# New slots for weight loads, weight splits and attention read-backs in a fused attention and feed-forward kernel

## The chip, the core and the metric

The kernel runs on one core of one Trainium2 chip. The core has a matrix engine (TensorE, PE in the profile, whose weight loads are a row of their own, PEld), a vector engine (DVE), an activation engine (ACT), a general engine (POOL) and an engine that issues most transfers (SP); 16 DMA engines move the data. The metric is the device time of the whole program in microseconds. All engines run their own instruction lists in order and wait for each other by semaphores, so the order of the instructions on each engine is part of the kernel.

## The reference

For 2048 tokens of width 576 the output is `x` plus an attention part plus a feed-forward part, both from the same normalised `x`:

```
xn = layernorm(x)
q, k, v = split(xn @ wqkv)                  # 32 heads of 18
# each token looks at 8 tokens: itself and those 2, 4, ... 14 before it
o = softmax(q . k_window * 18**-0.5) . v_window
out = x + o @ wo + relu(xn @ w1) @ w2       # w1: 576 x 4608, w2: 4608 x 576
```

Everything is float32. Since a token sees only tokens of its own parity, the even and the odd tokens are two independent problems up to the weights.

## The kernel before

**Tiling.** The program makes two phases, `ph` 0 and 1, one for each parity of 1024 tokens. In a phase the normalised tokens stand transposed in four tiles `XT` of 256 tokens (`xt_in` reads such a tile for phase 1, three transfers by `words_in`, L395 and L397; `xt_parts` splits it, L422 to L428). Each float32 operand is cut into a high and a low part, and a product is made of three: `two` writes the high part on ACT (L172) and the low part on DVE (L176) or, with `pooled`, on POOL (L174).

**Feed-forward.** The 4608 hidden columns are 36 blocks of 128. The first six come in two chunks `c` of three (`w1_load`, L188 and L193, brings one block `f` of a chunk with one transfer for 512 of the 576 rows and two for the last 64; `w1_split` cuts it). They are multiplied slot by slot: `h_two` makes the hidden values of one slot, `o_two` multiplies them with `w2`. The other 30 blocks are taken in 15 pairs by a Strassen scheme: a pair is two groups `g` of the 30 (`a` and `a + 1`), and each group has eight steps (`group`, `step`), in which TensorE alternates between hidden values (L163, `ph` and `pm`) and the product with `w2` (L163 or L142, `po`). A finished output piece is copied out of PSUM by ACT (L709, `ev`) and added to the output in DRAM by an accumulating transfer that POOL issues (L715, for rows of `wo` L718). `w2_load` (L207) brings a block of `w2` into one of two stage buffers `st2`, and `w2_split` cuts it in two halves; a load waits until the block two before it has been cut.

**Attention.** The heads go in four units of eight. Their products stand at groups 5, 11 and 17 (unit 0 in the slots before), the scores and sums run on DVE in the background (`bg`, `run_bg`). At the end of a unit DVE transposes the result (`o_turn`, L611 and L614) and SP writes it to DRAM (`o_out`, L619, four transfers). After the fourth unit the whole row block is read back as operands for `wo`: `ot_in` (L661, L663; three transfers for each of four row blocks `r0` to `r3`), `ot_split` (L670 on ACT, L671 and L672 on DVE; two halves for each block), and `wo_block` multiplies one block with `wo`. The rest of `wo` itself comes by `wo_rest` (L257, L260).

**What sets the order.** One Python pass writes all instructions. `on(ph, g, i, z, f)` hangs a call on step `i` of group `g`, "T" right behind the step's first matmuls, "O" behind its second ones; `at`, `first` and `late` do the same for slots. `run_bg` takes background work as far as a clock that the program itself keeps (`t["pe"]`, `t["dve"]`) leaves room. `ot_plan` makes a list of the read-back's calls, each with a condition and a distance in that clock to an earlier call, and `ot_go` takes the first that is allowed. Between the phases stands `seam()`: the last group of phase 0 (`tail_end`, `last_group`), the first slots of phase 1, and the multiplications with `wo`. After phase 1 `epilogue()` does the same without a successor. Nothing is reordered later; SP in particular issues transfers strictly in this order, and it waits with an issue when its buffer is not free or its data not there.

The calls around the change, in `plan_strassen` and `attention`:

```
on(ph, a - 1, 5, "O", w2_load, ph, f)
on(ph, a - 1, 6, "O", w2_load, ph, f + 1)
on(ph, a, 2, "O", w2_split, ph, f, (0,), True)
on(ph, a, 5, "T", w2_split, ph, f, (1,), True)
bg.append((NI * 160 + 150, o_turn, ()))
bg.append((0, o_out, ()))
```

Of the kernel before, what the change touches and what calls it, by code (L numbers as in the profile page):

```python
# [19 lines left out]
P = 128  # L20
# [50 lines left out]
def tile_body(ctx: ExitStack, tc: tile.TileContext, x, wqkv, wo, w1, w2, out):  # L71
# [112 lines left out]

    def w1_load(ph, c, f):
        st = ST[:, 640 * f : 640 * (f + 1)]
        cs = slice((c * C + f) * P, (c * C + f + 1) * P)
        nc.sync.dma_start(  # L188
            st[:, 0:512].rearrange("p (k c) -> p k c", k=KT),
            w1[0 : KT * P, cs].rearrange("(k p) c -> p k c", p=P),  # L190
        )
        for part in LOW, UPP:
            nc.sync.dma_start(st[part, 512:640], w1[KT * P : D, cs])  # L193

    def w1_split(ph, c, f, pooled=False):
        w = W1[ph, c, f] = w1_at(ph, c, f)
        two(w[:, 0, :], w[:, 1, :], ST[:, 640 * f : 640 * (f + 1)], 640, pooled)

# [336 lines left out]

    bg = deque()
    ready = {}

# [4 lines left out]
    def attention(ph, u):  # L543
# [498 lines left out]
    def plan_strassen(ph):  # L1042
        for p in range(NP):
            a = 2 * p
            f = NC0 * C + 2 * p
            if p:
# [32 lines left out]
        if ph == 0:  # L1079
            for i in range(2):  # L1080
                on(ph, NG - 1, 4 + i, "O", xt_in, 1, i)
            for i in range(2):
                on(ph, NG - 1, 8, "O" if i else "T", xt_parts, 1, i, 0)
                on(ph, NG - 1, 8, "O", xt_parts, 1, i, 1)
            on(ph, NG - 2, 6, "O", w1_load, 1, 0, 0)
            on(ph, NG - 2, 8, "O", w1_load, 1, 0, 1)
            on(ph, NG - 1, 2, "O", w1_load, 1, 0, 2)
            on(ph, NG - 2, 7, "O", w2_load, 1, 0)
            on(ph, NG - 1, 4, "O", w2_load, 1, 1)
            on(ph, NG - 1, 3, "O", w2_split, 1, 0, (0, 1), True)  # L1090
            on(ph, NG - 1, 6, "O", w1_split, 1, 0, 0, True)
            on(ph, NG - 1, 7, "O", w1_split, 1, 0, 1)

    OTQ, OTT = {}, {}

    def ot_plan(ph):
        z = OTQ[ph] = []
        done = lambda: ph in ready and t["pe"] > ready[ph] + 4.5
        free = lambda: done() and ("xs", ph) in hold
        z.append(("wl", wo_rest, (ph,), lambda: ph in ready, ()))  # L1100
# [77 lines left out]
    def group(ph, g):  # L1178
# [13 lines left out]
        def step(i, lower, upper, after, early=()):  # L1192
# [19 lines left out]
            fire(ph, g, i, "O")  # L1212
            ot_go(ph)
            for f, a in ins.pop((ph, g, i), ()):
# [58 lines left out]
    def seam():  # L1273
        ph, g, b = 0, NG - 1, BASE[1]

        def more(k):
            ot_go(0)
            if k == 2:
                for i in range(2, NTB):
                    xt_in(1, i)  # L1280
            elif k == 3:
                w2_load(1, 2)

        tail_end(0, more)
# [13 lines left out]
        w1_split(1, 0, 2, True)  # L1298
        w2_split(1, 2, pooled=True)
        wo_block(0, 0)  # L1300
# [14 lines left out]
    def epilogue():  # L1315
        ph = 1

        def more(k):
            ot_go(1)

# [48 lines left out]
    for ph in range(NPH):  # L1369
        b = BASE[ph]  # L1370
        for k in range(2 * NTB):
# [3 lines left out]
            qkv_slots.add(n)  # L1375
        for n, f in ((4, 0), (5, 1), (7, 2)):
            at(b + n, w1_load, ph, 1, f)
        for n, f in ((6, 0), (8, 1), (10, 2)):
# [26 lines left out]
        else:  # L1405
            for k in range(4):
                late(b + (0, 1, 3, 4)[k], xt_parts, 1, 4 + k, 0)
                late(b + (0, 1, 3, 4)[k], xt_parts, 1, 4 + k, 1)
            first(b + 3, wo_block, 0, 1)
# [31 lines left out]
    nc.scalar.activation(spare, mhalf, AF.Exp)  # L1441
    w1_load(0, 0, 0)
    load_x(2)
    w1_load(0, 0, 1)
    w1_load(0, 0, 2)
    w2_load(0, 0)
# [90 lines left out]
    for ph in range(NPH):  # L1537
        b = BASE[ph]
        for n in range(b + (FIRST if ph == 0 else 0), b + NOLD - 2):
# [5 lines left out]
            else:  # L1545
                h_two(g, n % 2 == 1)
            for f, a in todo.pop(n, []):
                f(*a)
# [11 lines left out]
        epilogue() if ph else seam()  # L1560
    assert not todo and not todo_late and not bg and not evs and not ins and not OTQ[0] and not OTQ[1]

# [25 lines left out]
```

## Time and profile before

| | |
|---|---|
| runs | 1141.21, 1142.63, 1145.81 us; median 1142.63 us |
| profiled execution | 1141.19 us, its span 1139.4 us, mean granted clock 0.993 |
| TensorE busy | 1112.4 us, 98% of the span |
| weight loads | 1097.7 us, 96% |
| VectorE, ACT, POOL | 75%, 50%, 34% |
| all DMA traffic | 177.27 MB, mean 156 GB/s |

A page of the profile is read from the span down: an engine that is busy 98% of the time bounds the kernel, and only its idle time and its slow clock can be won without taking work away. Times in the rows are microseconds from the span's start. In the rows of a timeline the last bracket says how long an engine stood idle ahead of the instruction and what ended the wait. "PEclk" is the clock that TensorE was granted, as a share of the full one. Phase 0 fills about the first half of the span; its last group begins near 514, and the last group of phase 1 near 1078.

### The profile page before, as it was taken

What the parts mean: (1) busy time and instruction counts of PE and PEld (TensorE: products, weight loads), DVE (VectorE), ACT (ScalarE), POOL (GpSimd) and SP (SyncE); (2) the same over time, 40 slices, a digit from 0 to 9 for tenths busy, and PEclk for the clock granted to TensorE, in tenths of its full rate; (3) what the DMA queues carried; (4) which work ended last, traced back from release to release, by engine and by line L of the source; (5) the groups of instructions that cost most, each with busy time, mean ns of one, the idle gap of its engine ahead of it and who ended that gap; (6) DMA issues with size and microseconds to landing.
All of it is one profiled execution on the core that took longest, in us unless ns stands there. A gap on an engine that the chain in (4) does not pass through costs nothing.

```text
span 1139.4 us, 37981 instructions
## 1 busy us (share of the span) xinstructions
PE 1112.4 (98%) x16410; PEld 1097.7 (96%) x16410; DVE 850.2 (75%) x1249; ACT 569.2 (50%) x1348; POOL 385.8 (34%) x382
## 2 busy tenths in 40 slices
PE   8999999999999999999999999999999999999988
PEld 8999999999999999998899999999999999999888
DVE  7676888898897898964316339987899989989441
ACT  4444564564464456656435245535645644655550
POOL 2313441343343344432212215333413423445221
PEclk9999999999999999999999999999999999999999
DMA  7469985794696498899857257759848947888885
GB/s 221 146 156 227 189 172 96 159 205 86 141 214 120 104 197 147 155 197 271 172 83 168 32 125 169 138 84 216 171 80 171 203 90 159 163 152 152 195 161 136
DMA packets 140727, 177.27 MB, mean 156 GB/s; under 512 B 28160, under 2 KB 88064, under 8 KB 140528
## 3 DMA queue, kind: packets, MB, share of 16 engines
q0 software_dynamic: 37632, 81.40, 45.6%
q1 hardware_dynamic: 102208, 92.55, 28.0%
q8 instruction: 129, 2.11, 0.7%
q10 hardware_dynamic: 720, 0.89, 0.2%
q14 instruction: 38, 0.31, 0.1%
HBM read 74.07 MB, written 96.22 MB: 149 GB/s over the span
## 4 chain that ended last, share of the span: by engine, by line
PE 85%; DVE 5%; DMA 4%; ACT 3%; issue 2%; SPq 1%; DVEq 0%; ACTq 0%; POOL 0%
PE po L163 28%; PE po L142 21%; PE ph L163 14%; PE pm L163 11%; PE pm L142 5%; PE ph L142 3%; DMA st<-in_w 2%; PE ph L130 1%; PE po L130 1%; DMA xS<-od 1%; DMA att<-od 1%; DVE ar L176 1%; ACT ar L172 1%; DVE att L611 1%; ACT ev L709 1%
## 5 line engine op out<-in xcount | busy, mean ns | idle before, releaser
L163 PE MATMUL po<-ar 64*128 64x320 f32 (+1 forms) x5760 | 484.0, 291 | 0.5 <-ACT ev L709 0.3
L163 PEld LDWEIGHTS po<-ar 64*128 64x128 f32 x5760 | 425.8, 185 | 2.1 <-ACT ev L709 0.5
L163 PE MATMUL ph<-xT,ar 64*128 64x256 f32 x2520 | 326.3, 277 | 9.1 <-ACT pm L979 5.5
L163 PEld LDWEIGHTS ph<-xT,ar 64*128 64x128 f32 x2520 | 291.3, 186 | 13.3 <-ACT pm L979 7.8
L715 POOL DMA_DIRECT2D out<-ev x128 | 152.8, 1194 | 415.5 <-ACT ev L709 333.0
L163 PE MATMUL pm<-xS,ar 64*128 64x256 f32 x2160 | 264.8, 277 | 0.6
L163 PEld LDWEIGHTS pm<-xS,ar 64*128 64x128 f32 x2160 | 241.4, 186 | 1.7 <-issue 0.9
L176 DVE TENSOR_TENSOR ar<-st,ar 128x256 fp32r<-128x256 f32 (+3 forms) x232 | 162.2, 703 | 98.5 <-ACT ar L172 86.7
L709 ACT ACTIVATE ev<-po 128x512 f32<-128x512 f32 (+1 forms) x266 | 171.1, 650 | 123.1 <-PE po L163 76.5
L172 ACT ACTIVATE ar<-st 128x256 fp32r<-128x256 f32 (+3 forms) x304 | 148.6, 502 | 28.8 <-DMA st<-in_w 22.1
L174 POOL TENSOR_TENSOR ar<-st,ar 128x256 fp32r<-128x256 f32 (+1 forms) x72 | 83.7, 1166 | 197.1 <-ACT ar L172 194.3
L142 PE MATMUL po<-wq,xT 64*128 64x432 f32 x1296 | 137.7, 353 | 0.0
L142 PEld LDWEIGHTS po<-wq,xT 64*128 64x128 f32 x1296 | 126.1, 184 | 0.4
L911 POOL TENSOR_TENSOR st<-st 128x256 f32<-128x256 f32 x120 | 120.3, 1007 | 17.7 <-DVE ar L760 7.1
L163 PE MATMUL ph<-xS,ar 64*128 64x256 f32 x720 | 103.2, 276 | 4.5 <-ACT ph L979 4.4
L163 PEld LDWEIGHTS ph<-xS,ar 64*128 64x128 f32 x720 | 94.6, 185 | 6.0 <-ACT ph L979 5.3
L564 DVE TENSOR_TENSOR pr<-att 128x1152 f32<-128x1152 f32 x64 | 92.2, 1453 | 0.1
L599 DVE TENSOR_TENSOR pr<-att 128x1152 f32<-128x1152 f32 x64 | 87.1, 1381 | 0.4
L567 DVE TENSOR_REDUCE att<-pr 128x64 f32<-128x1152 f32 x64 | 85.3, 1341 | 0.0
L606 DVE TENSOR_TENSOR pr<-pr 128x1152 f32<-128x1152 f32 x64 | 76.8, 1201 | 1.4
L142 PE MATMUL po<-ar 64*128 64x256 f32 (+1 forms) x984 | 72.0, 291 | 2.5 <-ACT ev L709 2.5
L142 PEld LDWEIGHTS po<-ar 64*128 64x128 f32 x984 | 66.6, 185 | 3.2 <-ACT ev L709 2.9
(121 smaller groups left out, 1327.6 us busy)
## 6 DMA issues: line engine op xcount, KB each, us to landing
out<-ev POOLq DMA_DIRECT2D x128, 576.0 KB, 7.0
st<-in_w SPq DMA_DIRECT2D x72, 288.0 KB, 5.2
st<-in_w SPq DMA_DIRECT2D x72, 256.0 KB, 3.7
att<-att SPq DMA_DIRECT2D x16, 441.0 KB, 4.6
att<-in_wqkv SPq DMA_DIRECT2D x28, 216.0 KB, 6.5
od<-att SPq DMA_DIRECT2D x32, 160.0 KB, 4.7
att<-in_x SPq DMA_DIRECT2D x14, 288.0 KB, 3.8
st<-in_w SPq DMA_DIRECT2D x60, 64.0 KB, 6.0
```

Source lines behind the costliest of these rows:

```text
L142: ins = nc.tensor.matmul(o, l[z], r[z], start=start, stop=stop)
L163: b.ins = nc.tensor.matmul(b.ap, l[part], r[part], start=start, stop=stop, skip_group_check=skip)
L172: nc.scalar.activation(hi, src, AF.Copy)
L174: nc.gpsimd.tensor_tensor(lo, src, f32(hi), op=ALU.subtract)
L176: nc.vector.tensor_tensor(lo, src, f32(hi), op=ALU.subtract)
L564: nc.vector.tensor_tensor(pr[i], q, window(k, i), op=ALU.mult)
L567: nc.vector.tensor_reduce(lg[:, i], pr.pop(i).rearrange(heads, d=Dh), axis=AX.X, op=ALU.add)
L599: nc.vector.tensor_tensor(pr[i].rearrange(heads, d=Dh), e, window(v, i).rearrange(heads, d=Dh), op=ALU.mult)
L606: nc.vector.tensor_tensor(o, z[:, :, 0:n], z[:, :, n : 2 * n], op=ALU.add)
L709: nc.scalar.activation(acc[:, :, cols], z[:, :, 0 : cols.stop - cols.start], AF.Copy)
L715: ADDED[ph, tb] = nc.gpsimd.dma_start(rows_of(ph, tb), acc, accum_op=ALU.add)
L911: nc.gpsimd.tensor_tensor(stg(o), stg(a), stg(b), op=op)
```

## The change

The arithmetic stays; what changes is when transfers and splits are issued.

- **W1.** A chunk of three blocks comes in one set of three transfers (128x4x384 and twice 64x384) in place of three sets; the first chunk of phase 0 keeps its nine (`w1_first`). The stage holds it in another order of dimensions.
- **Unit results.** `o_out` leaves the background list. It stands in `leaving` and is emitted once the program's clock is 2 us past `o_turn`.
- **W2 splits.** In each even group the POOL halves of block `f` move from steps 2 and 5 to steps 6 and 8. In the seam `w2_split(1, 0)` moves from step 3 of group 29 into `tail_end`, `w2_load(1, 2)` from the end of `tail_end` to its `more(1)`, and `w2_split(1, 2)` from the seam's end behind the second `o_two` of phase 1's slots.
- **Read-back.** Between the phases each `ot_in` now also waits for a mark (`hold["go", r]`): r0 for step 5 of group 29, r1 for `more(2)`, r2 and r3 for the first two slots of phase 1. Between two reads lie 3.0 in place of 5.0, between a read and its split 12.0 in place of 9.0 or 22.0. `ot_go` is called once in a step, no longer twice; in the epilogue's `more` 0, 0, 0 and 2 times.
- **x.** `xt_in(1, 3)` moves from `more(2)` into the first slot of phase 1; the parts of tiles 2 and 3 there go to slots 0, 1, 4, 5.

```
+    def w1_load(ph, c):
+        n = C * P
+        st, cs = ST[:, 0 : 5 * n].rearrange("p (k n) -> p k n", n=n), slice(c * n, (c + 1) * n)
+        nc.sync.dma_start(st[:, 0:KT], w1[0 : KT * P, cs].rearrange("(k p) c -> p k c", p=P))
+        for part in LOW, UPP:
+            nc.sync.dma_start(st[part, KT], w1[KT * P : D, cs])
...
+            leaving.append((t["pe"] + 2.0, o_out))
...
-        bg.append((0, o_out, ()))
...
+        while leaving and t["pe"] > leaving[0][0]:
+            leaving.popleft()[1]()
...
-                on(ph, a, 2, "O", w2_split, ph, f, (0,), True)
-                on(ph, a, 5, "T", w2_split, ph, f, (1,), True)
+                on(ph, a, 6, "T", w2_split, ph, f, (0,), True)
+                on(ph, a, 8, "T", w2_split, ph, f, (1,), True)
...
-            on(ph, NG - 2, 6, "O", w1_load, 1, 0, 0)
-            on(ph, NG - 2, 8, "O", w1_load, 1, 0, 1)
-            on(ph, NG - 1, 2, "O", w1_load, 1, 0, 2)
+            on(ph, NG - 1, 5, "O", hold.__setitem__, ("go", 0), True)
+            on(ph, NG - 2, 4, "O", w1_load, 1, 0)
...
-            on(ph, NG - 1, 3, "O", w2_split, 1, 0, (0, 1), True)
...
-            z.append((("in", r), ot_in, (ph, r), free if r == 3 else done, ((("in", r - 1), 5.0),) if r else (("wl", 6.0),)))
+            z.append((("in", r), ot_in, (ph, r), go(r), ((("in", r - 1), 3.0),) if r else (("wl", 6.0),)))
...
-                z.append((("split", r, h), ot_split, (ph, r, h), None, ((("in", r), 9.0 if ph or r == 0 else 22.0),)))
+                z.append((("split", r, h), ot_split, (ph, r, h), None, ((("in", r), 12.0),)))
...
-            if k == 2:
-                for i in range(2, NTB):
-                    xt_in(1, i)
-            elif k == 3:
+            if k == 1:
+                w2_split(1, 0, (0, 1), True)
                 w2_load(1, 2)
+            elif k == 2:
+                xt_in(1, 2)
+                hold["go", 1] = True
...
-        w2_split(1, 2, pooled=True)
         wo_block(0, 0)
...
+            late(b, w2_split, 1, 2, (0, 1), True)
```

In the changed file the same instructions stand some lines lower (L207 is L217 there, L619 is L631, L661 is L674, L670 is L683, L172 stays). TensorE's list is the same in both kernels, row for row.

SP's list at the end of phase 1, before. `od` is the DRAM buffer of the unit results, `st_...` a stage of `w2`, `att` the arena that takes `wo` and the read-back.

```order
L619 DMA od<-att 32x5x256 x4
L207 DMA st_20608<-in_w 128x576
L257 DMA att<-wo_143 128x576 x2
L260 DMA att<-wo_143 64x1x576 x2
L207 DMA st_20647<-in_w 128x576
L661 DMA att<-od 128x4x256
L663 DMA att<-od 64x1x256 x2
```

The same place after:

```order
L217 DMA st_20586<-in_w 128x576
L631 DMA od<-att 32x5x256 x4
L217 DMA st_20624<-in_w 128x576
L267 DMA att<-wo_143 128x576 x2
L270 DMA att<-wo_143 64x1x576 x2
L674 DMA att<-od 128x4x256
L676 DMA att<-od 64x1x256 x2
```

The first `w2` block now stands ahead of the unit's four writes, the second ahead of `wo`; in phase 0 the same rows are exchanged.

ACT's list in the last group of phase 0, before. `st_9796` is the second block of the last pair of phase 0, `st_10082` is block 0 of `w2` for phase 1.

```order
L172 ACTIVATE ar<-st_9796 128x320
L172 ACTIVATE ar<-st_10082 128x256
L172 ACTIVATE ar<-st_10082 128x320
L756 ACTIVATE ar<-pm 128x256
L979 ACTIVATE pm<-ph 128x256
L983 ACTIVATE m_10311<-pm 128x256
```

The same place after, where the two stages are called `st_9785` and `st_10066`:

```order
L172 ACTIVATE ar<-st_9785 128x320
L769 ACTIVATE ar<-pm 128x256
L992 ACTIVATE pm<-ph 128x256
L996 ACTIVATE m_10276<-pm 128x256
...
L769 ACTIVATE ar<-m_10276 128x256
L172 ACTIVATE ar<-st_10066 128x256
L172 ACTIVATE ar<-st_10066 128x320
L769 ACTIVATE ar<-pm 128x256
```

The split of block 0 moved from step 3 of group 29 to behind its step 8, past the copy L979 from which the matmuls of step 7 start.

ACT's list in the last group of phase 1, before; the L670 row is the split of read-back block r0, both halves.

```order
L983 ACTIVATE u_20943<-pm 128x256
L172 ACTIVATE wq<-att 128x576
L670 ACTIVATE att<-att 128x5x128 x2
L756 ACTIVATE ar<-u_20943 128x256
L756 ACTIVATE ar<-m_20882 128x256
L172 ACTIVATE ar<-st_20647 128x256
L979 ACTIVATE ph<-ph 128x256
```

The same place after:

```order
L996 ACTIVATE u_20921<-pm 128x256
L172 ACTIVATE ar<-st_20586 128x320
L172 ACTIVATE wq<-att 128x576
L769 ACTIVATE ar<-u_20921 128x256
L769 ACTIVATE ar<-m_20855 128x256
L172 ACTIVATE ar<-st_20624 128x256
L992 ACTIVATE ph<-ph 128x256
...
L769 ACTIVATE ar<-pm 128x256
L992 ACTIVATE pm<-ph 128x256
L683 ACTIVATE att<-att 128x5x128
```

The split of r0 moved from ahead of the copy of step 2 (`seed`, L979 with `ph`, now L992) to behind the copy of step 5 (`pm`).

More of the change, by code (lines that the diff above doesn't have):

```diff
@@ L183, in w1_at, with w1_stage, w1_first @@
         return AR[:, k : k + 1280].rearrange("p (z c) -> p z c", z=2)
[L185 to L191, printed above, removed]
-        for part in LOW, UPP:
-            nc.sync.dma_start(st[part, 512:640], w1[KT * P : D, cs])
+    def w1_stage(ph, c):
+        if ph == 0 and c == 0:
+            return ST[:, 0 : 5 * C * P].rearrange("p (f k c) -> p f k c", f=C, c=P)
+        return ST[:, 0 : 5 * C * P].rearrange("p (k f c) -> p f k c", f=C, c=P)
+    def w1_first(f):
+        st = w1_stage(0, 0)[:, f]
+        cs = slice(f * P, (f + 1) * P)
+        nc.sync.dma_start(st[:, 0:KT], w1[0 : KT * P, cs].rearrange("(k p) c -> p k c", p=P))
+        for part in LOW, UPP:
+            nc.sync.dma_start(st[part, KT], w1[KT * P : D, cs])
+    def w1_load(ph, c):
+        n = C * P
+        st, cs = ST[:, 0 : 5 * n].rearrange("p (k n) -> p k n", n=n), slice(c * n, (c + 1) * n)
+        nc.sync.dma_start(st[:, 0:KT], w1[0 : KT * P, cs].rearrange("(k p) c -> p k c", p=P))
+        for part in LOW, UPP:
+            nc.sync.dma_start(st[part, KT], w1[KT * P : D, cs])
     def w1_split(ph, c, f, pooled=False):
         w = W1[ph, c, f] = w1_at(ph, c, f)
-        two(w[:, 0, :], w[:, 1, :], ST[:, 640 * f : 640 * (f + 1)], 640, pooled)
+        hi, lo = (w[:, z, :].rearrange("p (k c) -> p k c", c=P) for z in range(2))
+        two(hi, lo, w1_stage(ph, c)[:, f], 640, pooled)
     def w2_at(ph, f, h):
@@ L536, in tile_body @@
     bg = deque()
+    leaving = deque()
     ready = {}
@@ L1099, in ot_plan, with go @@
         free = lambda: done() and ("xs", ph) in hold
+        def go(r):
+            if ph:
+                return free if r == 3 else done
+            return lambda: done() and ("go", r) in hold
         z.append(("wl", wo_rest, (ph,), lambda: ph in ready, ()))
@@ L1318, in more @@
         def more(k):
-            ot_go(1)
+            for _ in range((0, 0, 0, 2)[k]):
+                ot_go(1)
         tail_end(1, more)
@@ L1375, in tile_body @@
             qkv_slots.add(n)
-        for n, f in ((4, 0), (5, 1), (7, 2)):
-            at(b + n, w1_load, ph, 1, f)
+        at(b + 4, w1_load, ph, 1)
         for n, f in ((6, 0), (8, 1), (10, 2)):
@@ L1406, in tile_body @@
             for k in range(4):
-                late(b + (0, 1, 3, 4)[k], xt_parts, 1, 4 + k, 0)
-                late(b + (0, 1, 3, 4)[k], xt_parts, 1, 4 + k, 1)
+                late(b + (0, 1, 4, 5)[k], xt_parts, 1, 4 + k, 0)
+                late(b + (0, 1, 4, 5)[k], xt_parts, 1, 4 + k, 1)
+            at(b, xt_in, 1, 3)
+            at(b, hold.__setitem__, ("go", 2), True)
+            at(b + 1, hold.__setitem__, ("go", 3), True)
+            late(b, w2_split, 1, 2, (0, 1), True)
             first(b + 3, wo_block, 0, 1)
@@ L1441, in tile_body @@
     nc.scalar.activation(spare, mhalf, AF.Exp)
-    w1_load(0, 0, 0)
+    w1_first(0)
     load_x(2)
-    w1_load(0, 0, 1)
-    w1_load(0, 0, 2)
+    w1_first(1)
+    w1_first(2)
     w2_load(0, 0)
@@ L1560, in tile_body @@
         epilogue() if ph else seam()
-    assert not todo and not todo_late and not bg and not evs and not ins and not OTQ[0] and not OTQ[1]
+    assert not todo and not todo_late and not bg and not leaving and not evs and not ins and not OTQ[0] and not OTQ[1]
 def kernel(**inputs):
```

4 lines of the change are left out of this document (2 added, 2 removed).

## The prediction

> **What bounds the kernel.** I read the page first, then the busy time in stretches of 20 us, then what TensorE waits for, and then the rows around each of its long waits.
>
> ```profile
> span 1139.4 us, 37981 instructions
> ...
> PE 1112.4 (98%) x16410; PEld 1097.7 (96%) x16410; DVE 850.2 (75%) x1249; ACT 569.2 (50%) x1348; POOL 385.8 (34%) x382
> ...
> q0 software_dynamic: 37632, 81.40, 45.6%
> ...
> out<-ev POOLq DMA_DIRECT2D x128, 576.0 KB, 7.0
> ```
>
> TensorE is busy 98% of the span, so nothing can be won but the 2% in which it stands, and the time in which its clock is low. The next view is the busy time by stretches, for a stretch in the middle of phase 0 and those around the ends of the two phases (columns: length, busy time of PE, PEld, DVE, ACT, POOL, granted clock, DMA share, GB/s).
>
> ```profile
> 460.00:480.00 20.00, 20.00 (x328) 19.79 (x328) 19.46 (x29) 11.21 (x28) 8.38 (x9) 1.00 0.80 147
> ...
> 500.00:520.00 20.00, 18.75 (x298) 18.16 (x296) 9.96 (x20) 13.05 (x30) 5.23 (x6) 1.00 1.06 272
> 520.00:540.00 20.00, 17.33 (x237) 16.42 (x235) 7.18 (x15) 10.95 (x26) 6.69 (x6) 0.91 1.05 268
> 540.00:560.00 20.00, 17.51 (x250) 16.94 (x250) 5.93 (x15) 9.95 (x22) 7.34 (x7) 0.94 1.03 239
> 560.00:580.00 20.00, 19.74 (x306) 19.48 (x306) 7.41 (x16) 9.12 (x20) 3.01 (x3) 0.98 0.53 82
> ...
> 1060.00:1080.00 20.00, 18.10 (x265) 17.44 (x263) 7.88 (x16) 9.67 (x21) 5.18 (x5) 0.91 0.89 204
> 1080.00:1100.00 20.00, 16.57 (x228) 15.92 (x227) 10.60 (x24) 11.62 (x25) 2.87 (x3) 0.91 0.88 192
> ```
>
> In the middle TensorE is full and DVE nearly so; the loss lies at the two ends, and there the transfers are what is full. Now TensorE's own waits over the whole span (total, times, longest):
>
> ```profile
> PE ph L163 <- ACT pm L979: 5.5, 6, 2.5
> PE ph L163 <- ACT ph L979: 4.4, 4, 3.1
> PE po L142 <- ACT ev L709: 3.0, 3, 2.5
> PE ph L163 <- ACT ar L172: 1.6, 1, 1.6
> ...
> PE ph L163 <- DVE ar L760: 1.0, 3, 0.6
> ...
> PE ph L163 <- DVE ar L176: 0.7, 2, 0.3
> ```
>
> The long ones in its timeline:
>
> ```profile
> 511.12 0.39 PE L163 MATMUL ph<-xT,ar 64*128 64x256 f32 x1 [0.90 <-ACT pm L979]
> ...
> 525.72 0.38 PE L163 MATMUL ph<-xT,ar 64*128 64x256 f32 x1 [2.51 <-ACT pm L979]
> ...
> 556.22 1.67 PE L142 MATMUL po<-ar 64*128 64x256 f32 x16 [2.48 <-ACT ev L709]
> ...
> 1070.47 0.38 PE L163 MATMUL ph<-xT,ar 64*128 64x256 f32 x1 [1.56 <-ACT ar L172]
> ...
> 1085.06 0.39 PE L163 MATMUL ph<-xS,ar 64*128 64x256 f32 x1 [3.08 <-ACT ph L979]
> ```
>
> Five waits make 10.53 us. Each is for ACT, but ACT is only about half busy there; it is itself held up. Its timeline shows by what:
>
> ```profile
> 507.11 0.94 ACT L172 ACTIVATE ar<-st 128x256 fp32r<-128x256 f32 x2 [3.50 <-DMA st<-in_w]
> ...
> 523.70 0.78 ACT L172 ACTIVATE ar<-st 128x256 fp32r<-128x256 f32 x2 [3.66 <-DMA st<-in_w]
> ...
> 532.28 0.63 ACT L422 ACTIVATE xT<-xT 128x512 fp32r<-128x512 f32 x1 [2.44 <-DMA xT<-words]
> ...
> 554.90 0.78 ACT L172 ACTIVATE ar<-st 128x256 fp32r<-128x256 f32 x2 [8.10 <-DMA st<-in_w]
> ...
> 1069.48 0.93 ACT L172 ACTIVATE ar<-st 128x256 fp32r<-128x256 f32 x2 [5.13 <-DMA st<-in_w]
> ...
> 1071.57 0.69 ACT L172 ACTIVATE wq<-att 128x576 fp32r<-128x576 f32 x1 [0.28 <-DMA att<-wo]
> ...
> 1081.74 1.36 ACT L670 ACTIVATE att<-att 128x640 fp32r<-128x640 f32 x2 [4.07 <-DMA att<-od]
> ```
>
> Four times it is the split of a `w2` block that came late or was asked for early, once the split of read-back block r0; the waits for `x` (532.28) and `wo` (1071.57) cost TensorE nothing yet. SP's rows show when these were issued:
>
> ```profile
> 498.61 1.79 SPq L619 DMA_DIRECT2D od<-att  x4
> 500.50 0.41 SPq L207 DMA_DIRECT2D st<-in_w  x1
> ...
> 512.18 0.61 SPq L188 DMA_DIRECT2D st<-in_w  x1
> ...
> 514.71 0.68 SPq L207 DMA_DIRECT2D st<-in_w  x1
> ...
> 541.78 0.53 SPq L207 DMA_DIRECT2D st<-in_w  x1
> ...
> 1060.18 2.55 SPq L619 DMA_DIRECT2D od<-att  x4
> 1062.82 0.97 SPq L207 DMA_DIRECT2D st<-in_w  x1
> ...
> 1072.13 0.43 SPq L661 DMA_DIRECT2D att<-od  x1
> ```
>
> From issue to use: 500.50 to 507.11, 514.71 to 523.70, 541.78 to 554.90, 1062.82 to 1069.48, 1072.13 to 1081.74, that is 6.6, 9.0, 13.1, 6.7 and 9.6 us. Such latencies are a queue: the share of busy DMA time is 1.03 to 1.06 in 500 to 560. The largest single load in it are POOL's accumulations; 45.6% of 1139.4 us over 128 of them is 4.06 us of all 16 engines each, and the change leaves them alone.
>
> The low clock is the second loss. Every stretch that holds a wait of 1.5 us or more, or begins right behind one, shows 0.91 to 0.98, the others 1.00. One minus the clock times 20 us gives 1.8, 1.2 and 0.4 us in the seam (between the phases) and 1.8 and 1.8 us at the end of phase 1: 7.0 us.
>
> [...]
>
> **The change, part by part.** All sums stand against the profiled execution, 1141.19 us, which is 1.8 us outside and around its span and 1.4 us below the median of the three runs (1142.63).
>
> *W2 ahead of the unit's result.* In both phases `o_out` (L619) sat on SP until DVE's transposes were done, and the `w2` load behind it came 3.50 and 5.13 us late for ACT. Now the load stands ahead of the writes, behind nothing that waits, and the split is moved four steps back besides. The wait of 0.90 us at 511.12 and that of 1.56 at 1070.47 go, with two short ones for DVE's part of the same split (0.7 in the table): 3.2 us. The writes of `od` lose one load's issue, 0.4 to 1.0 us by the two L207 rows; what is late next is `wo`, which follows them, below.
>
> *The split of block 0 (seam).* It waited at step 3 of group 29 for a load issued at 514.71, and the copy L979 behind it held TensorE 2.51 us. Now it stands behind step 8, some five steps later. From step 7 of group 28 (511.12) to step 7 of group 29 (525.72) are 14.6 us, less the wait of 2.51 12.1, a step so about 1.5 us. ACT asked at 520.04 (523.70 less 3.66) and now asks five steps later and some 1.3 us earlier by the waits that went before, near 526. The load waits for its stage, which POOL's last split of the first block now frees at step 8 of group 28, so it goes out about when it did, and what landed at 523.70 is there at 526. The 2.51 us go.
>
> *The split of block 2 (seam).* Issue 541.78, asked for at 546.80 (554.90 less 8.10), landed 554.90. The load now stands ahead of two read-backs and two `x` tiles instead of behind them, and the split one slot pair later. Asked for later and issued earlier, each by several microseconds, it can bear 8.10 us; I take the whole 2.48 us of TensorE as gone. If only one of the two holds, a part of 2.48 stays.
>
> *The split of r0 at the end.* ACT asked at 1077.67, got it at 1081.74. It now stands behind the copy of step 5 rather than ahead of that of step 2: three steps or 4.5 us later, and with TensorE 1.9 us earlier ACT asks near 1080.3. If the read lands no earlier, ACT still waits 1.5 us. TensorE's wait was 1.0 us shorter than ACT's (3.08 against 4.07), so 0.5 of it may stay; I take 3.08 as gone and charge the 0.5 below.
>
> *The clock.* If the waits go, so do the 7.0 us, since no stretch without such a wait shows less than 1.00 in these rows.
>
> *W1 in three transfers.* Nine issues become three, all on SP, which is no bound; the first landed in time, and the blocks now come together. In the seam the set goes out ahead of the place of 512.18, where the first of nine was issued, and its split stays in steps 6 and 8 of group 29. Between 0 and a gain already counted through shorter queues; I take 0.
>
> *POOL halves at steps 6 and 8.* The same work lies beside other DVE instructions. What TensorE still waits outside the two ends bounds it from below: the waits table less the five rows leaves 2.1 (pm), 1.3 (ph), 0.5 (ev) and 1.0 (L760), 4.9 us in all, startup included. From above, as much again. I take 0 in between, as no row prefers a side.
>
> *New waits.* In the seam two transfers become tight once TensorE comes some 6 us earlier. Tile 0 of `x` already let ACT wait 2.44 us at 532.28, hidden; three read-backs no longer stand ahead of it, and W1 there takes three issues for nine. So 0 to 2.44, taken 0.5, near the lower end since fewer bytes are ahead of it. Block r0 there is now split right before `wo` needs it: 0 to 3.08 (the same read's wait at the other end), taken 0.4. At the end of phase 1, `wo` let ACT wait 0.28 us at 1071.57 when ACT was late by more than that; with TensorE 1.9 us ahead (0.28 + 1.9) 0 to 2.2, taken 0.5; and r0's 0.5 from above, 0 to 3.08. Together 1.9, between 0 and 10.8.
>
> Sum: 3.2 + 2.51 + 2.48 + 3.08 + 7.0 = 18.2 us won (3.2 is 0.90 + 1.56 + 0.7), less 1.9 = 16.3. The profiled execution comes to 1124.9, the median with its 1.4 us more to 1126.3; I say 1126.
>
> **The rivals.** A difference below 0.5% (5.7 us) is about what runs of this kernel cannot tell from no change.
>
> *One or two waits stay.* Transfers in the seam are still full (1.03 to 1.06), and every load only moves in the same queue. For it speaks the 13.1 us latency; against it, that each of the splits moved by more than its own wait. A wait that stays costs 2.5 to 3.1 us and 1.8 us of clock, so 4.3 to 4.9 each: 1130 to 1136.
>
> *The low clock is not bought with the waits.* If it falls for another cause at these places, only 11.2 less 1.9 us are won: 1141.2 − 9.3 + 1.4 gives 1133. [...] Against it: five of five dips stand with a wait.
>
> *DVE becomes the bound (slower).* POOL's halves slow the DVE instruction beside them, as the timeline of DVE and then of POOL shows in an even group, the same split ending ahead of POOL's start and beside it:
>
> ```profile
> 432.05 0.69 DVE L176 TENSOR_TENSOR ar<-st,ar 128x512 fp32r<-128x512 f32 x1
> ...
> 433.95 1.20 DVE L176 TENSOR_TENSOR ar<-st,ar 128x512 fp32r<-128x512 f32 x1
> ```
>
> ```profile
> 433.25 1.36 POOL L174 TENSOR_TENSOR ar<-st,ar 128x256 fp32r<-128x256 f32 x1 [2.64 <-ACT ar L172]
> ```
>
> The price is 0.5 us a meeting. With two in each of the 28 even groups it is 28 us if steps 6 and 8 lay it all on the hidden values that TensorE waits for, and steps 2 and 5 none. It decides from 58% of that on (16.3 of 28), and makes the kernel slower by 0.5% from 79% on; all of it gives 1154. For it: DVE has 0.54 us left in 460 to 480. Against: the meetings exist now, and TensorE waits for L760 1.0 us in the whole span.
>
> *It does not do what it says.* The reads wait for marks and longer distances; if that chain only shifts every wait by a slot, the time stays within 0.5% of 1142.6.
>
> **How the numbers follow.** Forecast, all five waits gone and small ones in their place (1120 to 1130): 0.60. One or two stay: 0.16. Clock stays low: 0.05. No difference: 0.08. Slower: 0.11, of which 0.02 within 0.5%. Faster by over 0.5%, that is below 1136.9, holds the first three: 0.81; same 0.08 + 0.02 = 0.10; slower 0.09. The lower end is the sum without new waits (1126.3 − 1.9) and with the 4.9 us of the middle gone, 1119.5. The upper end takes in two waits that stay, 1136. Outside lie the last two cases, 0.19.
>
> **What would show it.** Right: in the stretches 500 to 580 and 1060 to 1100 a granted clock of 1.00 and TensorE busy near 20 of 20; no wait of ACT's L172 for a `w2` load above 1 us; `w2` issued before `od` on SP; r0's split waiting under 1 us. The last `wo` products of phase 0 start about 10 us earlier. Wrong: a wait of TensorE above 1.5 us in those stretches, with `xT<-words`, `att<-od` or `att<-wo` behind it; or idle time spread in short pieces over 120 to 495, with DVE's L760 as what ended it; or a low clock without a wait.

## The result and the profile after

The changed kernel takes 1129.24 us (median of 4 runs, 1127.84 to 1130.19), the kernel before 1141.92 us in the same comparison; the ratio is 0.9886, with a 95% interval of 0.9854 to 0.9917. Forecast were 1126 us with a range of 1119 to 1136, so direction and range held. Of the 16.3 us that were to be won, 12.7 came by the medians; the profiled execution's span fell from 1139.4 to 1127.3 us, by 12.1.

The busy time by stretches, with the columns as before, now reads:

```profile
500.00:520.00 20.00, 20.00 (x333) 20.00 (x330) 10.52 (x21) 13.07 (x30) 5.51 (x6) 1.00 1.06 257
520.00:540.00 20.00, 19.94 (x304) 19.30 (x302) 8.76 (x20) 15.31 (x36) 8.22 (x8) 1.00 1.06 255
540.00:560.00 20.00, 19.74 (x304) 19.09 (x303) 7.84 (x16) 8.93 (x21) 6.83 (x7) 1.00 1.10 277
...
1060.00:1080.00 20.00, 17.66 (x266) 17.47 (x264) 7.81 (x14) 9.93 (x24) 4.60 (x5) 0.91 1.06 272
1080.00:1100.00 20.00, 19.15 (x279) 18.17 (x277) 8.89 (x19) 11.01 (x20) 4.81 (x4) 1.00 0.89 138
```

Between the phases TensorE is all but full and its clock whole, though the transfers are as crowded as before (1.06 to 1.10). At the end of phase 1 it isn't. TensorE's waits over the span:

```profile
PE pm L163 <- ACT u L996: 2.8, 2, 2.3
PE ph L163 <- ACT pm L992: 2.6, 6, 0.9
PE ph L163 <- DVE ar L773: 1.8, 3, 0.6
```

The waits of 2.51, 2.48, 3.08, 1.56 and 0.90 us are gone. New is one of 2.3 us, and the wait for DVE's L773 (L760 before) grew from 1.0 to 1.8 us. ACT's timeline shows what the new one hangs on; the copy `u` (L996) is what TensorE waits for:

```profile
1067.61 0.68 ACT L172 ACTIVATE wq<-att 128x576 fp32r<-128x576 f32 x1 [4.34 <-DMA att<-wo]
1068.20 0.69 ACT L722 ACTIVATE ev<-po 128x640 f32<-128x640 f32 x1
1068.78 0.38 ACT L996 ACTIVATE u<-pm 128x256 f32<-128x256 f32 x1
```

ACT stood 4.34 us at the split of the rest of `wo`, two instructions ahead of that copy. SP's timeline and, below it, SP's waits from 1050 to 1075 say why `wo` was late:

```profile
1052.88 2.37 SPq L631 DMA_DIRECT2D od<-att  x4
1055.35 0.80 SPq L217 DMA_DIRECT2D st<-in_w  x1
1063.07 0.83 SPq L267 DMA_DIRECT2D att<-wo  x2
```

```profile
SPq L267 <- DMA od<-att: 6.8, 1, 6.8
```

`wo` is read into the place from which the unit's result leaves, so it waits for the last of the four writes. POOL's timeline has an accumulation go out 0.42 us after the first of them:

```profile
1053.30 1.20 POOL L728 DMA_DIRECT2D out<-ev  x1 [4.09 <-ACT ev L722]
```

The two writes issued before it landed 2.3 and 3.4 us after their issue, the two behind it 8.3 and 8.1. The kernel before shows the same at this place: an accumulation at 1061.05 parts its four writes into two that took 2.9 us each and two that took 5.4 and 6.6. In phase 0 of the changed kernel the four writes were all issued before the next accumulation, none took over 4.0 us, and `wo` was there just in time. That the accumulation makes the writes slow is so argued from three places; no run took it away.

Since TensorE's list is the same in both kernels, the start of the same matmul can be compared through the span. TensorE's matmuls are counted here from the first, 0, to the last, 16409; the table gives by how much the same matmul starts later in the changed kernel (us, negative is earlier):

```
matmul   before at   after minus before
   300       42.3          +0.39
  6600      466.0          +1.56
  8100      572.0          -9.05
 12900      894.9          -8.97
 14700     1015.7          -8.09
 16409   (the last)       -12.06
```

The part between the phases brought 10.6 us, the end of phase 1 only 4.0, and the rest lost 2.5 us: 1.6 up to 466, of which 0.4 lie in the first 42 us, and 0.9 near 1010. Behind 572 a time of one kernel can be set beside a time of the other only less these 8 to 12 us.

### The profile page after: what moved, and what is told of

Its sections match the earlier page's. It is cut to its first block, busy times and chain, and to the rows that moved or that the text cites. A ratio compares the mean times of both kernels' runs of the same rounds, so it can differ in the third digit from the quotient of the medians.

```text
span 1127.3 us, 37950 instructions
## 1 busy us (share of the span) xinstructions
PE 1108.6 (98%) x16410; PEld 1093.4 (97%) x16410; DVE 850.8 (75%) x1249; ACT 571.0 (51%) x1348; POOL 367.9 (33%) x382
## 4 chain that ended last, share of the span: by engine, by line
PE 86%; DVE 6%; issue 3%; ACT 2%; DMA 2%; POOL 0%; DVEq 0%; ACTq 0%; POOLq 0%
PE po L163 28%; PE po L142 21%; PE ph L163 14%; PE pm L163 11%; PE pm L142 5%; PE ph L142 3%; PE ph L130 1%; DVE ar L176 1%; DVE ar L773 1%; PE po L130 1%; DMA out<-ev 1%; DVE pr L575 1%; DVE att L622 1%; ACT ev L722 1%; DVE pr L610 0%
## 5 line engine op out<-in xcount | busy, mean ns | idle before, releaser
L163 PE MATMUL po<-ar 64*128 64x320 f32 (+1 forms) x5760 | 473.9, 290 | 0.4 <-ACT ev L722 0.3
L163 PEld LDWEIGHTS po<-ar 64*128 64x128 f32 x5760 | 415.8, 185 | 2.0 <-ACT ev L722 0.6
L163 PE MATMUL pm<-xS,ar 64*128 64x256 f32 x2160 | 261.9, 276 | 3.5 <-ACT u L996 2.8
L176 DVE TENSOR_TENSOR ar<-st,ar 128x256 fp32r<-128x256 f32 (+3 forms) x232 | 155.6, 675 | 76.0 <-ACT ar L172 70.1
L172 ACT ACTIVATE ar<-st 128x256 fp32r<-128x256 f32 (+3 forms) x304 | 151.3, 503 | 12.1 <-PE po L142 3.5
L174 POOL TENSOR_TENSOR ar<-st,ar 128x256 fp32r<-128x256 f32 (+2 forms) x72 | 80.5, 1122 | 118.0 <-ACT ar L172 117.8
L924 POOL TENSOR_TENSOR st<-st 128x256 f32<-128x256 f32 x120 | 113.1, 948 | 15.2 <-DMA st<-in_w 10.9
L617 DVE TENSOR_TENSOR pr<-pr 128x1152 f32<-128x1152 f32 x64 | 68.8, 1075 | 1.4
L773 DVE SCALAR_TENSOR_TENSOR ar<-ph,ar 128x256 fp32r<-128x256 f32 x96 | 39.1, 418 | 39.9 <-ACT ar L769 39.5
```

Source lines behind the costliest of these rows:

```text
L163: b.ins = nc.tensor.matmul(b.ap, l[part], r[part], start=start, stop=stop, skip_group_check=skip)
L172: nc.scalar.activation(hi, src, AF.Copy)
L174: nc.gpsimd.tensor_tensor(lo, src, f32(hi), op=ALU.subtract)
L176: nc.vector.tensor_tensor(lo, src, f32(hi), op=ALU.subtract)
L617: nc.vector.tensor_tensor(o, z[:, :, 0:n], z[:, :, n : 2 * n], op=ALU.add)
L924: nc.gpsimd.tensor_tensor(stg(o), stg(a), stg(b), op=op)
```

## The experiments

Times are medians, ratios are against the kernel before in the same comparison.

### POOL's halves back at steps 2 and 5

```
-                on(ph, a, 6, "T", w2_split, ph, f, (0,), True)
-                on(ph, a, 8, "T", w2_split, ph, f, (1,), True)
+                on(ph, a, 2, "O", w2_split, ph, f, (0,), True)
+                on(ph, a, 5, "T", w2_split, ph, f, (1,), True)
```

> The changed kernel with the POOL halves of the W2 split back at steps 2 and 5 of every even group, all else as changed. Theory (the move itself costs time in the middle, because POOL's half at step 8 now runs with POOL's three sums behind it, and DVE's operations on the hidden values beside them took 1.25 and 0.96 us instead of 0.42 and 0.72): TensorE's two waits for DVE near 454 and 1005 fall from 0.56 and 0.59 us to the 0.18 of before, the time falls by 0.8 to 1.2 us; the ends of the phases stay as they are, since the loads still stand ahead of the unit's result. Rival (the later slot is what cured the wait near 511 and 1070): ACT waits for the w2 load again by 2 us or more, and the time rises by 2 to 6 us.

Measured: 1125.58 us, ratio 0.9841 (0.9799 to 0.9883), 3.7 us less where 0.8 to 1.2 were expected. The rival is out: no wait for `w2` came back. In the profiled execution, the slowest of the four (1127.92 us), the gain over the changed kernel is 0.86 us from matmul 6300 to 6600 and 0.87 from 14400 to 14700; the rest between the medians is not explained. Of the two waits for DVE one fell, from 0.59 to 0.18 us, the other only from 0.56 to 0.46. The mechanism is read from DVE's timeline. With the halves at steps 6 and 8 (the changed kernel):

```profile
443.05 1.25 DVE L773 SCALAR_TENSOR_TENSOR ar<-u,ar 128x256 fp32r<-128x256 f32 x1
444.23 0.96 DVE L773 SCALAR_TENSOR_TENSOR ar<-m,ar 128x256 fp32r<-128x256 f32 x1
```

With the halves back, the same two instructions:

```profile
443.59 0.42 DVE L773 SCALAR_TENSOR_TENSOR ar<-u,ar 128x256 fp32r<-128x256 f32 x1
444.16 0.72 DVE L773 SCALAR_TENSOR_TENSOR ar<-m,ar 128x256 fp32r<-128x256 f32 x1 [0.15 <-ACT ar L769]
```

POOL in the changed kernel works without a break beside them:

```profile
443.12 0.90 POOL L174 TENSOR_TENSOR ar<-st,ar 128x320 fp32r<-128x320 f32 x1
443.96 2.70 POOL L924 TENSOR_TENSOR st<-st 128x256 f32<-128x256 f32 x3
```

DVE loses 1.07 us there (1.25 + 0.96 less 0.42 + 0.72), 0.83 on the first instruction and 0.24 on the second, and TensorE, which has little slack in this group, most of it. One group of each phase pays; the 26 other even groups hide it. How much it is worth comes out more cleanly from the last pair of kernels below.

### wo's split later at the end of phase 1

```
-            z.append((("ws", kt), wo_split, (ph, kt), None, (("wl", 9 + 3.0 * (kt - 2)),)))
+            z.append((("ws", kt), wo_split, (ph, kt), None, (("wl", (14 if ph else 9) + 3.0 * (kt - 2)),)))
```

> The changed kernel with the split of the rest of wo allowed 5 us later in the program's clock at the end of phase 1 (14 in place of 9), nothing else. Theory (the wait of 2.34 us at 1068.9 comes from ACT standing 4.34 us at the split of wo, with the copy u behind it): the wait at 1068.9 goes below 0.5 us and the half clock behind it goes, so 3 to 4 us less than the changed kernel, about 1125.5. Rival (TensorE is held there by what is full anyway, transfers and DVE's part of the wo split): the wait moves to the next group's copies with the same size, and the time stays within 1 us of 1129.

Measured: 1130.2 us, ratio 0.9886 (0.9849 to 0.9922). The time is the rival's, but not by its mechanism: in 1060 to 1080 TensorE is now full, and the loss stands elsewhere.

```profile
1060.00:1080.00 20.00, 20.00 (x326) 19.84 (x326) 9.81 (x22) 12.94 (x29) 6.13 (x6) 1.00 1.07 266
1080.00:1100.00 20.00, 19.32 (x277) 18.32 (x275) 3.83 (x9) 7.56 (x13) 5.40 (x5) 1.00 0.89 159
1100.00:1120.00 20.00, 17.23 (x212) 15.67 (x210) 3.61 (x8) 2.67 (x4) 1.75 (x2) 0.91 0.61 135
```

Its timeline shows the place:

```profile
1113.92 0.41 PE L142 MATMUL po<-wq,xS 64*128 64x320 f32 x1 [2.07 <-ACT xS L683]
```

On ACT the split stands behind the output of the rows before it:

```profile
1113.13 1.36 ACT L683 ACTIVATE xS<-xS 128x640 fp32r<-128x640 f32 x2 [8.33 <-DVE xS L1362]
```

`ot_go` takes one call of the list at a time. The later split of `wo` used up calls that the list had given to the read-back, so the read of r3, from which its split's distance counts, came later in the program. On the chip it landed at 1084.7 us, hardly later than in the changed kernel (1084.2): it was the split's place in ACT's list that cost the 2.07 us, not the transfer. With 17 in place of 14 it was the same:

> The same with 17 in place of 9, so that the first part of wo is split some two steps later still. Theory: as with 14, and ACT waits for wo less than 0.5 us; time 1125 to 1126. Rival: the parts now fall among the read-back's splits, and the products with wo start late, 1 to 3 us above the kernel with 14.

Measured: 1130.61 us, ratio 0.9887, and the same wait for `xS` (2.07 us at 1113.6). ACT no longer waits for `wo`, as the theory had it, but the time did not follow. The rival's 1 to 3 us above the kernel with 14 did not come either (0.4 us); a late piece of the read-back was the cost already there.

So the next kernel also takes r3's read ahead of the splits in the list:

```
+        if ph:
+            z.insert(4, z.pop([e[0] for e in z].index(("in", 3))))
```

> The kernel with wo's split allowed 5 us later, and the last read (r3) put ahead of the other blocks' splits in the list of phase 1, so that its own split keeps its old place and doesn't fall behind the last multiplications, where it cost 2.07 us at 1113.6 in the run before. Theory: no wait over 1 us is left at the end of phase 1, no half clock there, 3 to 4 us less than the changed kernel: 1125 to 1126. Rival (the end of phase 1 is bound by transfers, each wait that goes comes back elsewhere): again within 1 us of 1129.

Measured: 1125.08 us, ratio 0.9857 (0.9823 to 0.9892), as the theory had it, and no stretch of 20 us from 1060 to 1120 has a clock below 1.00. `wo` itself lands no earlier, and ACT still waits 1.34 us for it; it only holds nothing that TensorE needs.

### W1 in nine transfers

```
+        for f in range(C):
+            z, at = st[:, :, f * P : (f + 1) * P], slice(cs.start + f * P, cs.start + (f + 1) * P)
+            nc.sync.dma_start(z[:, 0:KT], w1[0 : KT * P, at].rearrange("(k p) c -> p k c", p=P))
+            for part in LOW, UPP:
+                nc.sync.dma_start(z[part, KT], w1[KT * P : D, at])
```

> The changed kernel with each chunk of W1 read by nine transfers again, at the same place in SP's list. Theory (the number of transfers is worth nothing, the place is): time within 1 us of the changed kernel. Rival (SP's issues are scarce between the phases, where six more issues take about 4 us of SP): tile 0 of x lands 3 to 4 us later, ACT waits for it, and TensorE stands 1 to 3 us near 528, with a half clock behind it if it is the longer one: 1 to 5 us more.

Measured: 1128.34 us, ratio 0.9868 (0.9832 to 0.9904), within 1 us, and ACT does not wait for `x`. The one part of the change that lowers the count of transfers brings nothing that these runs show.

### The order of the unit's result and the w2 load

Undone in the changed kernel (`o_out` back in the background list):

> The changed kernel with the unit's result written straight behind the transposes again, so that the last unit's four writes stand ahead of the w2 load. The POOL halves stay at steps 6 and 8. Theory (either move alone is enough in phase 0: the split asks for the load four steps later than before): no wait of ACT for a w2 load in phase 0, at most 1 us in phase 1, time within 2 us of the changed kernel. Rival (the order of the load and the writes is what cured it): ACT's waits of 3.5 and 5.1 us return in both phases, with 0.9 and 1.6 us of TensorE, 3 to 5 us more.

Measured: 1132.43 us, ratio 0.9923 (0.9894 to 0.9951), 3.2 us more. Neither was right on the mechanism. No wait for `w2` came back; ACT waits for `wo` instead, 2.57 us in phase 0, where TensorE bears no wait above 0.45, and 6.59 in phase 1, with TensorE behind it:

```profile
1069.38 0.58 PE L163 MATMUL pm<-xT,ar 64*128 64x256 f32 x1 [3.75 <-ACT m L996]
```

The read-back's list counts its distances from the moment at which `o_out` is written into the program, and that moment is now 2 us of the program's clock earlier. So the first split of `wo` stands ahead of the copy `m` (L996) on ACT, four instructions above its place in the changed kernel, while `wo` lands no earlier.

Done alone, in the kernel before:

```
-        bg.append((0, o_out, ()))
...
+            leaving.append((t["pe"] + 2.0, o_out))
```

> The kernel before with one part of the change alone: the unit's result is written 2 us of the program's clock behind the transposes, so that the last unit's four writes come behind the w2 load. Theory (the order of that load and the writes was the cause of the waits near 511 and 1070): ACT's waits of 3.50 and 5.13 us for w2 go, with 0.90 and 1.56 us of TensorE and the half clock at 1073; at the end of phase 1 the wait for wo (2.3 us in the changed kernel) takes the place; 1 to 4 us less than before. Rival (without the later split the load is still late): no change, within 1 us.

Measured: 1134.56 us, ratio 0.9940 (0.9922 to 0.9958), 6.7 us less, more than the theory gave. TensorE's waits there:

```profile
PE ph L163 <- ACT pm L982: 4.2, 5, 2.2
PE pm L163 <- ACT m L986: 3.3, 1, 3.3
...
PE ph L163 <- ACT ph L982: 1.5, 4, 0.5
...
PE po L142 <- ACT ev L712: 0.5, 2, 0.3
```

The waits of 0.90 and 1.56 us are gone, and with them the two that I had put to other parts: 3.08 us for r0 and 2.48 us for block 2. The wait for block 0 (2.2) stays, and 3.3 us for `wo` are new. The edit does more than exchange a load and four writes: the whole read-back list counts from `o_out`, so the reads and splits behind it move as well. The read of r1 between the phases now stands behind a load of `w1`, and at the end of phase 1 the first half of r0's split stands three instructions later on ACT. ACT's stand at `wo` (5.75 us) also gives r0 time to land. Which of these ended the waits for r0 and block 2 was not tried apart.

### The splits between the phases

Block 0 back at step 3 of group 29:

```
-                w2_split(1, 0, (0, 1), True)
...
+            on(ph, NG - 1, 3, "O", w2_split, 1, 0, (0, 1), True)
```

> The changed kernel with the split of w2 block 0 of phase 1 back at step 3 of group 29. Theory (the split asked too early): ACT waits for that load 2.5 to 4 us, TensorE 1.5 to 3 us at step 7 with the copy behind it, and a half clock follows: 3 to 4.5 us more than the changed kernel. Rival (the load now comes earlier, or the slack behind it is enough): TensorE waits less than 0.5 us there and the time stays within 1 us.

Measured: 1130.99 us, ratio 0.9906 (0.9880 to 0.9932). ACT waits 2.69 us for the load, TensorE 2.30 us at 525.47, a half clock follows (0.50 from 526.11 to 529.52), and the span is 1130.8, 3.5 more than the changed kernel's: the mechanism is the theory's. The medians differ by only 1.75 us, less than its 3 to 4.5, and the intervals of the two ratios overlap; the profiled execution is the slowest of six, and two of the others have a mean clock of 1.000, hence no half clock after this wait.

Block 2, load and split, back at the old places:

```
-                w2_load(1, 2)
...
+            elif k == 3:
+                w2_load(1, 2)
...
-            late(b, w2_split, 1, 2, (0, 1), True)
...
+        w2_split(1, 2, pooled=True)
```

> The changed kernel with the load and the split of w2 block 2 of phase 1 both back at their old places (load at the end of the last group of phase 0, split ahead of the first products with wo). Theory (a load issued near 537 takes 9 to 14 us in this stretch, and ACT asks near 541): ACT waits 5 to 9 us for it, TensorE 1.5 to 2.5 us near 546, and if 1.35 us of that fall into one window of the clock's grid a half clock follows: 2 to 4.5 us more than the changed kernel. Rival (with the earlier waits gone the load lands in time): within 1 us.

Measured: 1130.3 us, ratio 0.9913 (0.9879 to 0.9947), 1.1 us more by the medians. ACT waits 6.84 us, as expected, but TensorE only 0.69 at 550.01, and no half clock follows (the mean clock is 1.000). The 1.35 us of the expectation is what TensorE stood idle in the kernel before from 1069.46 to 1072.87, ahead of a half clock (its row is in the last section). The rival's size was nearer, though not for its reason.

### The marks of the read-back

```
-            return lambda: done() and ("go", r) in hold
+            return free if r == 3 else done
```

> The changed kernel without the marks: between the phases r0, r1 and r2 are read as early as the list allows, ahead of block 0 of w2 and of the tiles of x. Theory (what goes first in a full queue is there first, so the reads push block 0 and tile 0 of x back by three reads, 3 to 6 us): ACT waits for tile 0 or 1 of x, TensorE 1 to 4 us near 528 to 540, with a half clock 3 to 6 us more than the changed kernel. Rival (the reads are small beside the accumulations, order among the loads is worth little): within 1 us.

Measured: 1138.11 us, ratio 0.9972 (0.9952 to 0.9991): 8.9 us above the changed kernel, more than the theory's 3 to 6. TensorE's long waits there:

```profile
526.89 0.38 PE L163 MATMUL pm<-xS,ar 64*128 64x256 f32 x1 [1.15 <-ACT u L996]
...
536.30 0.58 PE L142 MATMUL ph<-xT,ar 64*128 64x256 f32 x1 [5.01 <-ACT xT L432]
...
541.36 1.83 PE L163 MATMUL po<-ar 64*128 64x320 f32 x24 [1.08 <-ACT ev L722]
```

SP issues tile 0 of `x` (L405) only behind nine transfers of the read-back:

```profile
524.21 0.43 SPq L405 DMA_DIRECT2D xT<-words  x1
```

In the changed kernel:

```profile
516.25 0.62 SPq L405 DMA_DIRECT2D xT<-words  x1
```

Of the parts undone one at a time, this one cost most.

### r0's split at the end of phase 1

```
-            for _ in range((0, 0, 0, 2)[k]):
-                ot_go(1)
+            ot_go(1)
...
-                z.append((("split", r, h), ot_split, (ph, r, h), None, ((("in", r), 12.0),)))
+                z.append((("split", r, h), ot_split, (ph, r, h), None, ((("in", r), 9.0 if ph else 12.0),)))
```

> The changed kernel with the read-back's splits of phase 1 in their old slots (distance 9.0, one call in each part of the last group's end). Theory (r0 landed at 1071.71 and its split began only at 1076.54, so the late slot was not what cured this wait): TensorE waits no more than 0.5 us longer there and the time stays within 1 us of the changed kernel. Rival (the prediction's reason, the later slot): ACT waits 2 us or more for r0 again, TensorE 1 to 3 us, with a half clock 3 to 5 us more.

Measured: 1129.54 us, ratio 0.9897 (0.9872 to 0.9923), the same as the changed kernel, and ACT doesn't wait for r0 at all. So the place behind the copy of step 5 is not needed. But the distances of before do not bring back the place of before: there r0's split stood ahead of the copy of step 2 (`ph`), here it still stands behind it:

```profile
1072.88 0.36 ACT L992 ACTIVATE ph<-ph 128x256 f32<-128x256 f32 x1
...
1074.23 0.73 ACT L683 ACTIVATE att<-att 128x640 fp32r<-128x640 f32 x1
```

The last part of r0 landed at 1071.81. In the old place, ahead of the instruction of 1069.93 on ACT, ACT would have stood for some 1.9 us (an estimate from these two times, against 4.07 before). That a later slot is no part of the cure is therefore not shown. Nor is the earlier slot free: two later waits of TensorE for ACT, 0.51 and 0.28 us in the changed kernel, are 0.91 and 0.92 here, with splits of the read-back ahead of the copies it waits for.

### Both corrections

> The same, and the POOL halves of the W2 split back at steps 2 and 5. If both effects are real and independent, 1 us (the waits for DVE near 454 and 1005) and 3 to 4 us (the end of phase 1) add up: 1124 to 1125, below the changed kernel by 4 to 5 us. If the one run so far with the POOL halves back (1125.6) owed its gain to the end of phase 1 as well, less adds up: about 1125.5.

Measured: 1122.38 us (6 runs, 1121.62 to 1125.18), ratio 0.9835 (0.9803 to 0.9867). It beats both kernels, by 2 us more than was expected. Against the kernel with only the end of phase 1 corrected (1125.08), the same matmuls gain 0.86 us from 6300 to 6600 and 0.87 us from 14400 to 14700: this is what POOL's halves at steps 6 and 8 cost, once in each phase, 1.7 us in all. The rest of the 2.7 us lies in small shifts, the largest (0.65) at the end of phase 1, and was not followed.

## Why the prediction was right, and where it was not

**The five waits.** All five went, as forecast, with the clock behind them. The comparison of the same matmuls shows 10.6 us between the phases; the sum had 9.6 there (0.35, 0.90, 2.51, 2.48 and 3.4 of clock), less 0.9 of new waits. So 1.9 us more came than were forecast, 0.9 because the new waits stayed away and 1.0 in TensorE's busy time, for a reason that no run shows; without them the forecast would have missed by 5 us and not by 3, and that it came closer is luck. At the end of phase 1 it had 8.6 (1.56, 0.34, 3.08 and 3.6 of clock) less 1.0, and 4.0 came. Block 0's reason (asked too early) is shown by putting it back. Two steps gave a move more credit than it had. The step on r0 set three steps of delay against a wait of 4.07 us. The read left 7 us earlier (1065.17 for 1072.13), but TensorE is 7.5 us ahead there, so that is no gain; what changed besides the slot is that r0 took 6.5 us from its first issue to its last landing, not 9.5. A slot just behind the copy of step 2 was late enough; how much of the wait the slot took away and how much the quicker read stays open. The step on block 2 gave its own move the credit for 2.48 us; put back, it costs TensorE 0.69, and the part on the unit's result alone already takes the wait away in the kernel before. I had costed each wait by its own load and its own split, though all share one queue.

**New waits, the step that was mis-sized.** For `wo` the prediction had 0 to 2.2 us and took 0.5, since the row of before showed 0.28. In the profiled execution it measured 2.34, above the upper end, and a half clock followed (0.50 from 1069.00 to 1072.41), 1.7 us, of which the term had none: 4 us in place of 0.5. A wait of TensorE above 1.5 us with `att<-wo` behind it was one of the signs that the prediction had named for being wrong. That this wait is the loss is shown by the kernel that splits `wo` later and reads r3 sooner. Nothing of the kind came between the phases, where 0.9 was charged. The bound was taken from ACT's delay at one row; it left out that `wo` cannot be issued before the unit's result has left, which SP's waits of before, from 1055 to 1090, showed as 5.0 us:

```profile
SPq L257 <- DMA od<-att: 5.0, 1, 5.0
```

**POOL's halves, also mis-sized.** Taken at 0 between -4.9 and +4.9, they cost 1.7 us. The rival that turned this into a slower kernel had the right mechanism, and its price of 0.5 us a meeting is about what the two instructions show (0.83 and 0.24 us), but one group of 14 in each phase exposes it, not 58% of them.

**W1** was taken at 0, and putting its nine transfers back shows no difference beyond the scatter. **The rivals:** 1129.24 lies at the upper edge of the forecast's own 1120 to 1130, beside "one or two waits stay"; what was found is one new wait with another cause. That the low clock has a cause other than the waits is out: it went with them (1.00 from 500 to 560), and came back with the one for `wo` (0.91 in 1060 to 1080). That the marks might shift each wait by a slot is refuted: without them 8.9 us are lost. The 4.06 us of an accumulation, which no sum uses, are a little high: 16 more transfers of the same queue are in the 45.6%, and by bytes (75.5 of 81.4 MB) it is 3.8 us.

## What to carry to other kernels

Where the transfers are full and TensorE is nearly so, list for each wait what stands in the same queue ahead of it, not only its own load: letting one store, and the reads that are timed from it, go out 2 us later took away four waits here and brought one of 3.3 us, and a group of reads at the wrong place cost 8.9 us. A split that may have to wait belongs behind the copies that the matmuls need, not ahead of them: ACT's stand of 4.34 us at the split of `wo` held TensorE 2.34 us. When a planner gives out one call at a time, moving one entry moves the others too, so the lists of all engines should be compared after each edit, and times of two kernels only after taking off how far one is ahead.

## What the runs showed of the chip

In the profiled execution of the kernel before the clock fell to 0.50 at 526.74, 557.46, 1072.87 and 1086.52 us, each time for 3.41 us; the distances, 30.72, 515.41 and 13.65 us, are 9, 151 and 4 times 3.413. If the span is laid out in stretches of this length that start where the clock fell, the falls in these rows go with TensorE's idle time inside one stretch and not with the length of a wait. Stretches of the kernel before and the ones behind them (columns as above):

```profile
523.33:526.74 3.41, 1.02 (x16) 1.02 (x18) 0.85 (x2) 2.49 (x8) 1.54 (x2) 1.00 1.13 273
526.74:530.15 3.41, 3.41 (x34) 3.41 (x32) 0.60 (x1) 2.26 (x4) 1.86 (x2) 0.50 1.07 311
...
1069.46:1072.87 3.41, 2.06 (x22) 1.59 (x24) 1.81 (x3) 3.10 (x8) 1.92 (x2) 1.00 0.67 222
1072.87:1076.28 3.41, 3.41 (x34) 3.41 (x33) 1.36 (x3) 2.28 (x6) 0.86 (x1) 0.50 0.95 179
```

And of the kernel with block 0's split put back, around a wait of 2.24 us that lies in two stretches:

```profile
1068.80:1072.21 3.41, 2.21 (x40) 2.01 (x36) 0.00 (x0) 0.56 (x1) 0.00 (x0) 1.00 0.89 289
1072.21:1075.62 3.41, 2.37 (x36) 2.37 (x38) 2.64 (x3) 2.22 (x6) 2.12 (x2) 1.00 1.08 336
```

With 2.39 and 1.35 us idle in a stretch (3.41 less busy) the next one ran at half clock; with 1.20 and 1.04 it didn't (the second row above has 1.00, and that execution's mean clock, 0.998 over 1130.8 us, has room for one half clock of 3.41 us, the one at 526.11), though that wait of 2.24 us was longer than the one of 1.56 behind the 1.35. In the profiled executions of the kernel before and of the changed kernel, outside the first 20 and the last 6 us, the five stretches with 1.35 us idle or more (2.39, 2.17, 1.35 and 1.95 before, 2.13 after) were followed by a half clock and none of the others, with 1.14 us or less; what happens between 1.14 and 1.35, or in another kernel, these two do not show. Of two waits of nearly one length, the 2.34 us of the changed kernel thus had 1.7 us more behind them (half of 3.41, an estimate) and the 2.24 us nothing. The scatter between executions fits this: of the changed kernel's four, the one with a mean clock of 1.000 has a span of 1126.1 us, the three with 0.998 have 1127.3 to 1128.4.
